# The opening of an adaLN block: Q/K weights loaded first, and chunk 2's norm, Q/K and values put elsewhere in the order

## The chip, the cores and the metric

The kernel runs on one core of one Trainium2 chip. The metric is the device time of one execution in microseconds (us), as the median of the runs. Before the change it is 575.89 us (three runs, 574.8 to 576.01).

## The reference

One transformer block on 2048 rows of 576 numbers: a modulation from a condition c, a local attention (32 heads of 18, 8 keys at a distance of 2 rows each), and a feed-forward of 4608 features. Cut to what matters:

```python
mod = (silu(c) @ w_mod).reshape(6, -1)           # sa, ca, ga, sb, cb, gb
h = layernorm(x) * (1 + ca) + sa
q, k, v = split(h @ wqkv)                        # 32 heads of 18
idx = pos - 2 * [0..7]                           # rows before 0 are masked
attn = softmax((q . k[idx]) * 18 ** -0.5)
x = x + ga * ((attn . v[idx]) @ wo)
h = layernorm(x) * (1 + cb) + sb
x = x + gb * (((h @ w_gate) * (h @ w_up)) @ w_down)
```

## The kernel before

The rows are cut into eight chunks of 256 (CH), each of two tiles of 128 rows (ST = 2). The feed-forward takes the 16 tiles in five groups (GROUPS): 2, 4, 4, 3 and 3 tiles. For each group `gate_up` walks through 36 feature blocks of 128 (FT) on TensorE, with the attention of later chunks as background pieces on the other engines, and `down` accumulates the output, with Q/K/V of later chunks between its matmuls.

The change is in what comes before the first `gate_up`, the opening. It has to bring the attention of chunk 0 to its end (x1, the second layernorm, and its transposed form h2T), the Q, K and V of chunks 1 and 2, and the modulation columns and rows. The order of work is written by hand (`manual_schedule` for all engines): each engine runs its instructions in the order in which the program issues them, and waits where an operand or a buffer isn't ready. So the order of the Python calls at lines 729 to 881 is the order of each engine's queue.

The names in that order:

- `load_x`, `load_k`, `load_wgu`, `load_res` (L130 to L169) issue DMAs on SP's queue. `wqk` holds the weights of Q and K, `wv` those of V. At L191 to L197 the queue has w_mod's first two blocks, x of chunk 1, `wv`, then `wqk`.
- `a_ln(i)` (L306) takes the layernorm sums of chunk i on VectorE (L233, L235); `aa[i]["rsq"]()` makes 1/sqrt on ScalarE (L238, L239); `aa[i]["norm"]()` normalizes on VectorE (L243); `a_norm(i)` is both. `a_t(i)` transposes the chunk on TensorE (L270) and applies the modulation while evicting (L259 on VectorE, L261 on ScalarE) into hT, of which there is one buffer.
- `a_qj(j, g, ...)` makes Q and K of tile j of chunk 0 (L338), in three groups of tiles: g = 0 is Q without its last tile, g = 1 the tile that Q and K share, g = 2 the rest of K. `a_q(i, g)` does so for both tiles of a later chunk in five groups. Both evict on ScalarE (L341 to L346). `a_v(i, j)` makes V (L364, L366), evicted on ScalarE (L368, L369). For later chunks it is written to the DRAM tile vd by POOL's queue (L375).
- `pj(j, w)` multiplies Q by the K that is shifted for window place w on VectorE (L761, six product buffers), `lj(j, w)` sums it by head on TensorE (L769); `max_j`, `sum_j` are the softmax (L775 to L777, L783 to L785).
- `to_keys(j)` turns the weights from queries to keys (L481, L484; copied by ScalarE, L487), `av_mul(j, hf)` weights V on VectorE (L496), `av_sum(j, hf)` sums with shifted matmuls into the three PSUM banks po (L507), copied to oT by ScalarE (L510 to L512).
- `b_wj(j)` is the output projection of tile j (L521); the function that it returns adds the residual and takes the sums of the second layernorm (L527, L528, L233). `rsq2`, `norm2` and `transposed(xn2, ...)` then make h2T, which the first gate/up matmuls (L621) read.
- `mod_columns(wmB, 1)` and `mod_row(...)` make modulation columns and the row of ga (L283; L295, L297, L298).
- `b_ld(i, j)` gathers the value rows of eight window places from vd into vsh, on POOL's queue (L383), `behind` makes it wait for the landing of a load of gate/up weights. The first group's `gate_up` reads chunk 1's vsh in its second half (L449).

PSUM has eight banks. In the opening, five are a rotating pool (psp0, `ps`), three hold po. When the opening ends both pools close, and a pool of all eight opens for `gate_up`.

Of the kernel before, what the change touches and what calls it, by code (L numbers as in the profile page):

```python
# [12 lines left out]
PSUM = bass.MemoryType.PSUM  # L13
# [6 lines left out]
D = 576  # L20
# [23 lines left out]
def kernel(  # L44
# [40 lines left out]
    wdp = pool("wdp", 3)  # L85
    gup = pool("gup", 3)
    outr = pool("outr", 1)
    guards = [tc.tile_pool(name="psp0", bufs=5, space=PSUM), tc.tile_pool(name="pop", bufs=3, space=PSUM)]
    psp, pop = [g.__enter__() for g in guards]

    def ps(shape, dt, name):
        return psp.tile(shape, dt, name=name, tag="bank")
# [1 line left out]
    def js(j):  # L94
        return slice(j * P, (j + 1) * P)
# [34 lines left out]
    def load_x(i):  # L130
        if i < NCH:
            x_in[i] = sp.tile([P, ST, D], BF, name="x_t1") if i == 1 else xin.tile([P, ST, D], BF, name="x_t")
            nc.sync.dma_start(x_in[i][:], x_rows(i))
# [32 lines left out]
    def load_k(dst, wsrc, c0, n):  # L166
        r = nc.sync.dma_start(dst(slice(0, P), slice(0, KF)), wsrc[0:KF * P, c0:c0 + n].rearrange("(k p) n -> p k n", p=P))
        nc.sync.dma_start(dst(slice(0, 64), KF), wsrc[KF * P:D, c0:c0 + n])
        return r  # L169
# [20 lines left out]
    nc.gpsimd.memset(wmCr[64:, :], 0.0)  # L190
    load_wm(wmA, 0, 0)  # L191
    load_wm(wmA, 1, 1)
    load_x(1)
    load_k(lambda p, k: wv[p, k, :], A_wqkv, 2 * D, D)
    load_k(lambda p, k: wqk[p, k, 0:D], A_wqkv, 0, D)
    load_k(lambda p, k: wqk[p, k, D:DP], A_wqkv, 2 * D - 64, 64)
    load_k(lambda p, k: wqk[p, k, DP:2 * D], A_wqkv, D, D - 64)  # L197


    nc.gpsimd.memset(ident[:], 0.0)  # L200
# [77 lines left out]
    def mod_columns(wm, pi):  # L278
        pm = ps([P, 2, KT], F32, "pm")
        for bi in range(2):  # L280
            for kt in range(KT):
                for m in range(KT):
                    nc.tensor.matmul(pm[:, bi, m:m + 1], lhsT=wm[:, kt, bi, col(m)], rhs=sc[:, kt:kt + 1],  # L283
                                     start=(bi == 0 and kt == 0 and m == 0), stop=(kt == KT - 1), skip_group_check=True)
        c01 = slice(2 * pi, 2 * pi + 2)
        nc.vector.tensor_tensor(modc[:, c01, 0:KF], pm[:, :, 0:KF], addc[:, :, 0:KF], ALU.add)
        for r in (slice(0, 64), slice(64, P)):
            nc.vector.tensor_tensor(modc[r, c01, KF:KT], pm[64:P, :, KF:KT], addc[64:P, :, KF:KT], ALU.add)
# [17 lines left out]
    def a_ln(i):  # L306
        x = x_in.pop(i)
        xn, rsq, norm = layernorm(lambda j: x[:, j, :], "a")
        aa[i] = dict(xn=xn, rsq=rsq, norm=norm)

    def a_norm(i):
        aa[i]["rsq"]()
        aa[i]["norm"]()
# [11 lines left out]
    def a_t(i, on_dve=True):  # L325
        a_tiles(i)
        hT = aa[i]["hT"]
        transposed(aa[i]["xn"], lambda m: hT[:, m, :], (0, 1), 0)(on_dve)
# [19 lines left out]
    def a_q(i, g):  # L348
        qk_tiles(i, QGRP[g], slice(0, CH), nc.scalar.copy)
        if g == 2:  # L350
            a_halo(i)

    def a_qj(j, g, evict):
        qk_tiles(0, QGRPJ[g], js(j), evict)
# [4 lines left out]
    def a_v(i, j):  # L359
        hT = aa[i]["hT"]  # L360
        pv = ps([P, VA * DH], F32, "pv")
        pvr = ps([P, VR * DH], F32, "pvr")
        for kt in range(KT):
            nc.tensor.matmul(pv[:], lhsT=hT[:, kt, js(j)], rhs=wv[:, kt, 0:VA * DH], start=(kt == 0), stop=(kt == KT - 1))  # L364
        for kt in range(KT):
            nc.tensor.matmul(pvr[:], lhsT=hT[:, kt, js(j)], rhs=wv[:, kt, VA * DH:D], start=(kt == 0), stop=(kt == KT - 1))  # L366
        v_sb = vstage.tile([P, DH, H], BF, name="v_sb")[:] if i else v0(j)
        nc.scalar.copy(v_sb[:, :, 0:VA], pv[:].rearrange("p (h d) -> p d h", d=DH))  # L368
        nc.scalar.copy(v_sb[:, :, VA:H], pvr[:].rearrange("p (h d) -> p d h", d=DH))  # L369
        r0 = HALO + i * CH + j * P  # L370
        if i == 0:
            if j == 1:
                nc.gpsimd.dma_start(vd[r0 + P - HALO:r0 + P, :], o_sbs[0][P - HALO:P, j, 0:D])
            return
        nc.gpsimd.dma_start(vd[r0:r0 + P, :], v_sb.rearrange("p d h -> p (d h)"))  # L375
# [116 lines left out]
    def av_mul(j, hf):  # L492
        if hf == 0:
            weighted.append(vshp.tile([P, W, DH, H], BF, name="vsh"))
        ws = slice(4 * hf, 4 * hf + 4)
        nc.vector.tensor_tensor(weighted[j][:, ws], v0(j)[:, None].to_broadcast([P, 4, DH, H]),  # L496
                                keyed[j][:, ws, None, :].to_broadcast([P, 4, DH, H]), ALU.mult)

    def av_sum(j, hf):
        if j == 0 and hf == 0:  # L500
            pos.extend(pop.tile([P, 2, CH], F32, name="po") for _ in range(3))
        v = weighted[j][:].rearrange("p w d h -> p w (d h)")
        r = DIL * (W - 1) if j == 0 else 0
        for w in range(4 * hf, 4 * hf + 4):
            sh = DIL * (W - 1 - w)
            for m in range(KT):
                nc.tensor.matmul(pos[m // 2][:, m % 2, j * P:(j + 1) * P + r], lhsT=v[:, w, col(m)], rhs=slide[:, P - sh:2 * P - sh + r],  # L507
                                 start=(j == 0 and w == 0 and m % 2 == 0), stop=(w == W - 1), skip_group_check=True)
        if hf == 1:
            nc.scalar.copy(oT[:, 0:2, js(j)], pos[0][:, :, js(j)])  # L510
            nc.scalar.copy(oT[:, 2:4, js(j)], pos[1][:, :, js(j)])
            nc.scalar.copy(oT[0:64, KF, js(j)], pos[2][64:P, 0, js(j)])  # L512
# [234 lines left out]
    mod_columns(wmA, 0)  # L747
    for e in ev:
        e()
    a_ln(1)  # L750
    for j in range(ST):
        for g in range(3):
            a_qj(j, g, nc.scalar.copy)

    prods, lgs = {}, {}
    dd0 = smp.tile([P, ST, W, H], F32, name="dd")
# [1 line left out]
    def pj(j, w):  # L758
        off = HALO - DIL * (W - 1 - w) + j * P
        prods[j, w] = prodp.tile([P, KT, P], BF, name="prodj", tag="prod")  # L760
        nc.vector.tensor_tensor(prods[j, w][:], aa[0]["qT"][:, :, js(j)], aa[0]["kT"][:, :, off:off + P], ALU.mult)  # L761

    def lj(j, w):
        if w == 0:
            lgs[j] = ps([P, W, H], F32, "lgj")
            if j == 0:
                nc.tensor.matmul(lgs[j][:], lhsT=ident[:], rhs=maskneg[:], start=True, stop=False, skip_group_check=True)
        for m in range(KT):
            nc.tensor.matmul(lgs[j][:, w, :], lhsT=prods[j, w][:, m, :], rhs=ind[:, m, :],  # L769
                             start=(m == 0 and j == 1), stop=(m == KT - 1), skip_group_check=True)  # L770

    def max_j(j):
        dd = dd0[:, j]
        mx = small.tile([P, H], F32, name="mxj")
        nc.vector.tensor_reduce(mx[:], lgs[j][:].rearrange("p w h -> p h w"), axis=AX.X, op=ALU.max)  # L775
        nc.vector.tensor_tensor(dd, lgs[j][:], mx[:, None, :].to_broadcast([P, W, H]), ALU.subtract)
        nc.scalar.activation(dd, dd, ACTF.Exp, scale=scale)  # L777
# [26 lines left out]
    for g in range(5):  # L804
        load_wgu(g)

    for w in range(2):
        pj(0, w)
    a_norm(1)
    for w in range(2, 4):  # L810
        pj(0, w)
    for w in range(4):
        lj(0, w)
        pj(0, w + 4)
    a_v(0, 0)
    for w in range(4, 8):
        lj(0, w)
    a_v(0, 1)
    for w in range(2):
        pj(1, w)  # L820
    max_j(0)
    for w in range(2, 4):
        pj(1, w)
    a_t(1, False)
    for w in range(4):
        lj(1, w)
    for w in range(4, 6):
# [1 line left out]
    sum_j(0)  # L829
    for w in range(6, 8):  # L830
        pj(1, w)
    a_q(1, 0)
    a_q(1, 1)
    for w in range(4, 8):
        lj(1, w)
    max_j(1)
    mod_columns(wmB, 1)
    a_q(1, 2)
    sum_j(1)
    a_q(1, 3)  # L840
    for j in range(ST):
        to_keys(j)
    av_mul(0, 0)
    a_q(1, 4)
    a_v(1, 0)
    av_mul(0, 1)
    av_sum(0, 0)
    a_v(1, 1)
    a_ln(2)
    aa[2]["rsq"]()  # L850
    av_sum(0, 1)
    av_mul(1, 0)
    aa[2]["norm"]()
    mod_row(lambda p, k: wmC[p, k, :] if k < KF else wmCr[p, :], ga_bc, sc_bc)
    x1_half = b_wj(0)
    av_sum(1, 0)
    av_mul(1, 1)
    a_t(2, False)
    xn2, stat2, rsq2, norm2 = ln_parts(lambda j: x1[0][j], "b")
    x1_half(stat2)  # L860
    rsq2(slice(0, 1))
    av_sum(1, 1)
    a_q(2, 0)
    x1_half = b_wj(1)
    behind(b_ld(1, 0), wgu_in[0])
    behind(b_ld(1, 1), wgu_in[1])
    x1_half(stat2)
    rsq2(slice(1, 2))
    norm2(0)
    ht, _ = h2_of(0)  # L870
    a_q(2, 1)
    transposed(xn2, lambda m: ht[:, m, js(0)], (0,), 2)()
    norm2(1)
    a_q(2, 2)
    a_q(2, 3)
    transposed(xn2, lambda m: ht[:, m, js(1)], (1,), 2)()
    a_q(2, 4)
    for j in range(ST):
        a_v(2, j)
    load_res(1)  # L880
    load_x(4)
    for guard in [sp_guard] + guards[::-1]:
# [73 lines left out]
```

## Time and profile before

| what | us |
|---|---|
| median of three runs | 575.89 |
| profiled execution | 575.69 |
| its span, first to last instruction | 573.7 |
| first Q/K matmul (L338) | 14.45 |
| first gate/up matmul (L621) | 63.06 |
| TensorE busy, whole span | 547.6 (95%) |
| VectorE, ScalarE, POOL busy | 327.1, 250.9, 67.2 |

The span in 40 slices of 14.3 us (busy tenths; 9 is 90% or more) shows the first four slices, the opening and a little more, apart from the rest:

```profile
PE   1897999999999999999999999999999999999996
DVE  5477679896667787343667777505727614322202
ACT  2354666444455555233255565131366611455500
PEclk9899999999999999999999999999999999999999
DMA  9999596958444665364433874338646665665063
```

The row PEclk is the clock that the throttle granted to TensorE. The DMA engines are full for the first four slices. Times of single events are us from the start of the span.

### The profile page before, as it was taken

To read this page: it belongs to the slowest core of one execution; us is meant where nothing else is said; L and a number is where in the kernel's file an instruction comes from. 1 tells how busy PE (TensorE), PEld (TensorE's weight loads), DVE (VectorE), ACT (ScalarE), POOL (GpSimd) and SP (SyncE) were. 2 spreads that over 40 slices of the span, in tenths; PEclk is the share of its full clock that TensorE was granted. 3 is DMA by queue.
4 is the path that set the end of the run, shared out by engine and by line. 5 is a ranking of instruction groups with operands and counts; after the bars stand their busy time and mean duration, and the time that the engine had idled before them with its cause. 6 is when DMAs were issued, how large, how long until landed. Compare 5 with 4: busy or idle time off the path is not lost.

```text
span 573.7 us, 14145 instructions
## 1 busy us (share of the span) xinstructions
PE 547.6 (95%) x5959; PEld 321.0 (56%) x5959; DVE 327.1 (57%) x787; ACT 250.9 (44%) x576; POOL 67.2 (12%) x103
## 2 busy tenths in 40 slices
PE   1897999999999999999999999999999999999996
PEld 1676888566444445656444444565556555565553
DVE  5477679896667787343667777505727614322202
ACT  2354666444455555233255565131366611455500
POOL 7001300222100100131100000122000022000020
PEclk9899999999999999999999999999999999999999
DMA  9999596958444665364433874338646665665063
GB/s 255 279 272 363 169 285 207 345 160 277 129 146 135 223 218 174 119 207 146 145 112 110 264 237 147 97 92 294 192 149 176 211 200 167 186 187 183 1 173 106
DMA packets 72303, 108.13 MB, mean 188 GB/s; under 512 B 4752, under 2 KB 62176, under 8 KB 72112
## 3 DMA queue, kind: packets, MB, share of 16 engines
q1 hardware_dynamic: 60464, 61.42, 35.3%
q0 software_dynamic: 11168, 45.81, 25.5%
q8 instruction: 46, 0.75, 0.6%
q14 instruction: 17, 0.14, 0.1%
q10 hardware_dynamic: 608, 0.00, 0.1%
HBM read 102.78 MB, written 4.44 MB: 187 GB/s over the span
## 4 chain that ended last, share of the span: by engine, by line
PE 82%; issue 3%; DMA 3%; DVE 0%; POOL 0%; ACT 0%; SPq 0%; POOLq 0%; DVEq 0%
PE pg L621 25%; PE acc L685 21%; PE pu L621 20%; PE pq L338 4%; PE accr L690 3%; PE pw L538 2%; PE pv L364 2%; PE lg L399 1%; DMA wd<-in_B_w_down_dram 1%; DMA wgu<-in_B_w_up_dram 1%; PE tr_pA L270 1%; PE oT_pA L469 0%; PE tr_pB L270 0%; PE pwr L536 0%; POOL vsh L383 0%
## 5 line engine op out<-in xcount | busy, mean ns | idle before, releaser
L621 PE MATMUL pg<-h2T,wgu 64*128 64x512 bf16 (+2 forms) x1440 | 277.3, 333 | 0.0
L621 PE MATMUL pu<-h2T,wgu 64*128 64x512 bf16 (+2 forms) x1440 | 276.0, 333 | 0.0
L621 PEld LDWEIGHTS <-wgu 64*128 64x128 bf16 x2880 | 141.4, 94 | 107.1 <-issue 0.5
L685 PE MATMUL acc<-wd,hh 128*128 128x512 bf16 x576 | 149.4, 380 | 0.5 <-DMA wd<-in_B_w_down_dram 0.4
L645 ACT CAST u_sb<-pu 128x512 bf16<-128x512 f32 (+2 forms) x180 | 90.1, 501 | 136.5 <-PE pg L621 133.1
L650 DVE TENSOR_TENSOR hh<-g_sb,u_sb 128x512 bf16<-128x512 bf16 (+2 forms) x180 | 66.2, 369 | 102.6 <-ACT g_sb L646 97.8
L690 PE MATMUL accr<-wd,hh 128*128 128x64 bf16 x576 | 101.0, 193 | 0.0
L646 ACT CAST g_sb<-pg 128x512 bf16<-128x512 f32 (+2 forms) x180 | 91.4, 508 | 0.0
L685 PEld LDWEIGHTS <-hh 128*128 128x128 bf16 x576 | 56.0, 98 | 62.7 <-issue 1.7
L164 POOL DMA_DIRECT2D wd<-in_B_w_down_dram x45 | 33.8, 752 | 282.7 <-PE accr L690 230.0
L621 PE MATMUL pg<-h2T,wgr 64*128 64x512 bf16 (+2 forms) x180 | 60.2, 335 | 0.6 <-ACT v_sb L369 0.6
L621 PE MATMUL pu<-h2T,wgr 64*128 64x512 bf16 (+2 forms) x180 | 60.2, 335 | 0.3 <-ACT u_sb L645 0.3
L690 PEld LDWEIGHTS <-hh 128*128 128x128 bf16 x576 | 52.4, 98 | 2.9 <-issue 0.9
L338 PE MATMUL pq<-hT,wqk 128*128 128x256 bf16 (+1 forms) x405 | 46.7, 268 | 5.0 <-DMA wqk<-in_A_wqkv_dram 4.3
L389 DVE TENSOR_TENSOR prod<-qT,kT 128x1280 bf16<-128x1280 bf16 x56 | 44.7, 818 | 2.8 <-PE lg L399 2.8
L338 PEld LDWEIGHTS <-wqk 128*128 128x128 bf16 x405 | 35.6, 102 | 11.4 <-DMA wqk<-in_A_wqkv_dram 4.3
L449 DVE TENSOR_TENSOR vsh<-vsh,attn 128x1152 bf16<-128x1152 bf16 x56 | 40.9, 750 | 0.0
L259 DVE TENSOR_SCALAR h2T<-tr_pA,modc 128x256 bf16<-128x256 bf16 (+1 forms) x30 | 9.7, 377 | 36.8 <-PE tr_pA L270 36.8
L383 POOL DMA_DIRECT2D vsh<-vd x14 | 12.6, 901 | 140.7 <-DVE o_sb L460 88.0
L621 PEld LDWEIGHTS <-wgr 64*128 64x128 bf16 x360 | 18.1, 94 | 17.3 <-issue 4.8
L341 ACT CAST qT<-pq 128x512 bf16<-128x512 f32 x16 | 9.3, 582 | 34.9 <-PE pq L338 34.9
L364 PE MATMUL pv<-wv,hT 128*128 128x504 bf16 x80 | 20.9, 395 | 0.0
(149 smaller groups left out, 435.6 us busy)
## 6 DMA issues: line engine op xcount, KB each, us to landing
wd<-in_B_w_down_dram POOLq DMA_DIRECT2D x45, 576.0 KB, 4.6
wgu<-in_B_w_gate_dram SPq DMA_DIRECT2D x45, 512.0 KB, 4.0
wgu<-in_B_w_up_dram SPq DMA_DIRECT2D x45, 512.0 KB, 5.2
vsh<-vd POOLq DMA_DIRECT2D x14, 1152.0 KB, 7.3
x_r<-in_A_x_dram SPq DMA_DIRECT2D x8, 288.0 KB, 6.3
out_dram<-x SPq DMA_DIRECT2D x16, 144.0 KB, 4.3
x_t<-in_A_x_dram SPq DMA_DIRECT2D x7, 288.0 KB, 6.3
vd<-v_sb POOLq DMA_DIRECT2D x14, 144.0 KB, 2.9
```

The costliest lines, as they stand in the source:

```text
L164: return nc.gpsimd.dma_start(wb[:], B_w_down[r0:r0 + FB * P, :].rearrange("(k p) n -> p k n", p=P))
L338: nc.tensor.matmul(pq[:, gi, :], lhsT=wqk[:, kt, m * P:(m + 1) * P], rhs=hT[:, kt, cols], start=(kt == 0), stop=(kt == KT - 1))
L364: nc.tensor.matmul(pv[:], lhsT=hT[:, kt, js(j)], rhs=wv[:, kt, 0:VA * DH], start=(kt == 0), stop=(kt == KT - 1))
L383: return nc.gpsimd.dma_start(vsh[:].rearrange("p w d h -> p w (d h)"), vsrc)
L389: nc.vector.tensor_tensor(prod[:], aa[i]["qT"][:], aa[i]["kT"][:, :, off:off + CH], ALU.mult)
L449: nc.vector.tensor_tensor(v, v, at, ALU.mult)
L621: return nc.tensor.matmul(bank[:, 0:N], lhsT=lhs, rhs=rhs, start=first, stop=last, skip_group_check=True)
L645: nc.scalar.copy(u[:, 0:N], pu[:, 0:N])
L646: nc.scalar.copy(g[:, 0:N], pg[:, 0:N])
L650: nc.vector.tensor_tensor(hh[:, f, 0:N], gu[0][:, 0:N], gu[1][:, 0:N], ALU.mult)
L685: nc.tensor.matmul(acc[j][:], lhsT=hh[:, f, js(j)], rhs=wb[:, f % FB, 0:512], start=(f == 0), stop=(f == FT - 1))
L690: nc.tensor.matmul(accr[:, j, :], lhsT=hh[:, f, js(j)], rhs=wb[:, f % FB, 512:D], start=(f == 0 and j == 0), stop=(f == FT - 1), skip_grou ...
```

## The change

The order of the opening is rewritten; no computation is added or left out. On SP's queue the six loads of `wqk` go ahead of x of chunk 1 and of `wv`. Q of both tiles of chunk 0 is made before K. The sums of chunk 1's layernorm come after chunk 0's Q/K, and its 1/sqrt directly behind them. V of chunk 0 is made early, ahead of chunk 1's transposes. Chunk 2's sums stand before the second softmax maximum, its norm before the second softmax sum, its transposes and ga's row before `to_keys`. The four `av_mul` follow each other but for Q/K groups of chunk 2 on TensorE. V of chunk 2 comes before the last transposes. The gathers of chunk 1's value rows are issued last, behind loads 3 and 4 of the gate/up weights and no longer 0 and 1. The three banks po are allocated below the five of psp0.

```diff
-    guards = [tc.tile_pool(name="psp0", bufs=5, space=PSUM), tc.tile_pool(name="pop", bufs=3, space=PSUM)]
-    psp, pop = [g.__enter__() for g in guards]
+    guards = [tc.tile_pool(name="pop", bufs=3, space=PSUM), tc.tile_pool(name="psp0", bufs=5, space=PSUM)]
+    pop, psp = [g.__enter__() for g in guards]
...
-    load_x(1)
-    load_k(lambda p, k: wv[p, k, :], A_wqkv, 2 * D, D)
     load_k(lambda p, k: wqk[p, k, 0:D], A_wqkv, 0, D)
     load_k(lambda p, k: wqk[p, k, D:DP], A_wqkv, 2 * D - 64, 64)
     load_k(lambda p, k: wqk[p, k, DP:2 * D], A_wqkv, D, D - 64)
+    load_x(1)
+    load_k(lambda p, k: wv[p, k, :], A_wqkv, 2 * D, D)
...
+    for j, g in ((0, 0), (1, 0), (0, 1), (0, 2), (1, 1), (1, 2)):
+        a_qj(j, g, nc.scalar.copy)
     a_ln(1)
-    for j in range(ST):
-        for g in range(3):
-            a_qj(j, g, nc.scalar.copy)
+    aa[1]["rsq"]()
...
-    for w in range(2):
+    for w in range(3):
         pj(0, w)
-    a_norm(1)
-    for w in range(2, 4):
+    aa[1]["norm"]()
+    for j in range(ST):
+        a_v(0, j)
+    for w in range(3, 6):
         pj(0, w)
+    a_t(1, False)
     for w in range(4):
         lj(0, w)
-        pj(0, w + 4)
-    a_v(0, 0)
+    for w in range(6, 8):
+        pj(0, w)
+    a_q(1, 0)
     for w in range(4, 8):
         lj(0, w)
-    a_v(0, 1)
-    for w in range(2):
+    for w in range(4):
         pj(1, w)
     max_j(0)
-    for w in range(2, 4):
-        pj(1, w)
-    a_t(1, False)
+    a_q(1, 1)
+    a_q(1, 2)
     for w in range(4):
         lj(1, w)
     for w in range(4, 6):
...
-    a_q(1, 0)
-    a_q(1, 1)
+    a_q(1, 3)
     for w in range(4, 8):
         lj(1, w)
+    a_ln(2)
+    aa[2]["rsq"]()
     max_j(1)
+    a_q(1, 4)
     mod_columns(wmB, 1)
-    a_q(1, 2)
+    aa[2]["norm"]()
     sum_j(1)
-    a_q(1, 3)
+    for j in range(ST):
+        a_v(1, j)
+    a_t(2, False)
+    mod_row(lambda p, k: wmC[p, k, :] if k < KF else wmCr[p, :], ga_bc, sc_bc)
     for j in range(ST):
         to_keys(j)
     av_mul(0, 0)
-    a_q(1, 4)
-    a_v(1, 0)
     av_mul(0, 1)
+    a_q(2, 0)
     av_sum(0, 0)
-    a_v(1, 1)
-    a_ln(2)
-    aa[2]["rsq"]()
+    av_mul(1, 0)
+    a_q(2, 1)
     av_sum(0, 1)
-    av_mul(1, 0)
-    aa[2]["norm"]()
-    mod_row(lambda p, k: wmC[p, k, :] if k < KF else wmCr[p, :], ga_bc, sc_bc)
+    av_mul(1, 1)
+    xn2, stat2, rsq2, norm2 = ln_parts(lambda j: x1[0][j], "b")
+    ht, _ = h2_of(0)
+    av_sum(1, 0)
     x1_half = b_wj(0)
-    av_sum(1, 0)
-    av_mul(1, 1)
-    a_t(2, False)
-    xn2, stat2, rsq2, norm2 = ln_parts(lambda j: x1[0][j], "b")
     x1_half(stat2)
     rsq2(slice(0, 1))
+    a_q(2, 2)
     av_sum(1, 1)
-    a_q(2, 0)
+    norm2(0)
+    a_q(2, 3)
     x1_half = b_wj(1)
-    behind(b_ld(1, 0), wgu_in[0])
-    behind(b_ld(1, 1), wgu_in[1])
     x1_half(stat2)
     rsq2(slice(1, 2))
-    norm2(0)
-    ht, _ = h2_of(0)
-    a_q(2, 1)
     transposed(xn2, lambda m: ht[:, m, js(0)], (0,), 2)()
     norm2(1)
-    a_q(2, 2)
-    a_q(2, 3)
-    transposed(xn2, lambda m: ht[:, m, js(1)], (1,), 2)()
     a_q(2, 4)
     for j in range(ST):
         a_v(2, j)
+    transposed(xn2, lambda m: ht[:, m, js(1)], (1,), 2)()
+    behind(b_ld(1, 0), wgu_in[3])
+    behind(b_ld(1, 1), wgu_in[4])
     load_res(1)
     load_x(4)
```

## The prediction

> **What bounds the kernel now.** The first view to read is that of the waits of TensorE (PE). From 62 us to the end it has 1.8 us in all:
>
> ```profile
> PE pg L621 <- ACT v_sb L369: 0.6, 1, 0.6
> PE pwr L536 <- ACT oT L470: 0.5, 1, 0.5
> PE acc L685 <- DMA wd<-in_B_w_down_dram: 0.4, 1, 0.4
> PE pu L621 <- ACT u_sb L645: 0.3, 1, 0.3
> ```
>
> So from the first gate/up matmul (L621, at 63.06) on, PE sets the time, and whatever moves that start moves the end. The opening before it is the opposite. The same view up to 63.05, longest waits:
>
> ```profile
> PE tr_pA L270 <- DVE ln_xn L243: 7.7, 2, 6.3
> PE pq L338 <- DMA wqk<-in_A_wqkv_dram: 4.3, 1, 4.3
> PE lgj L769 <- DVE prodj L761: 2.4, 1, 2.4
> PE pwj L521 <- ACT oT L510: 1.9, 1, 1.9
> ```
>
> The 4.3 is Q/K's wait for weights, which ends at 14.45. Busy time by stretch (length, then PE, PEld, DVE, ACT, POOL, granted clock, DMA share, GB/s) says what limits what follows:
>
> ```profile
> 14.44:21.36 6.92, 6.91 (x94) 6.83 (x95) 0.89 (x2) 2.81 (x7) 0.00 (x0) 1.00 1.10 306
> 21.36:31.20 9.84, 6.83 (x93) 4.18 (x92) 7.48 (x20) 3.85 (x11) 0.66 (x1) 0.83 1.10 238
> 31.20:38.34 7.14, 6.55 (x131) 5.97 (x130) 4.88 (x14) 3.69 (x10) 0.00 (x0) 1.00 1.03 250
> 38.34:46.45 8.11, 8.11 (x89) 6.05 (x88) 8.04 (x14) 4.23 (x13) 1.11 (x2) 1.00 1.09 353
> 46.45:52.54 6.09, 4.17 (x62) 3.64 (x60) 3.20 (x9) 2.29 (x7) 1.81 (x2) 1.00 1.09 366
> 56.20:63.06 6.86, 5.91 (x56) 4.45 (x57) 4.18 (x12) 5.73 (x16) 0.57 (x1) 1.00 0.36 126
> ```
>
> PE alone in Q/K; then VectorE (DVE) and PE by turns; in the last stretch ScalarE (ACT) is near full, and its timeline shows the end of the opening:
>
> ```profile
> 56.64 0.57 ACT L341 CAST qT<-pq 128x512 bf16<-128x512 f32 x1
> 57.10 0.81 ACT L261 ACTIVATE h2T<-tr_pB,modc 128x128 bf16<-128x128 bf16 x2
> 57.94 0.37 ACT L343 CAST kT<-pq 64x256 bf16<-64x256 f32 x1
> ...
> 62.31 0.58 ACT L368 CAST v_sb<-pv 128x504 bf16<-128x504 f32 x1 [0.53 <-PE pv L364]
> 62.78 0.23 ACT L369 CAST v_sb<-pvr 128x72 bf16<-128x72 f32 x1
> ```
>
> Chunk 2's Q/K and V evictions stand there behind the last layernorm and end at 63.01.
>
> **The change, step by step.** I walk the new order through the engines; every duration is start to next start in the timelines of before. "(before x)" is the same event there.
>
> 1. Q/K weights first. 288 KB of x1 and 648 KB of wv leave the place before them: 0.96 MB at 340 to 299 GB/s (slices 5 to 10 and 10 to 15 us) is 2.8 to 3.2 us; I take 3.0, so Q starts at 11.45 (before 14.45). Its hT tiles are there: DVE evicts from 10.80, ACT is done at 11.95. The cost falls on what moved back: 1.33 MB of wqk passes x1, which lands at 10.3 + 4.3 = 14.6; its sums (1.9) end at 16.5, under Q/K. wv lands ahead of x2, whose place in the queue is unchanged (12.2 + 5.5 = 17.7); it is needed at 18.2. Were it 2 us later still, a_v(0) would only meet the transposes that wait for chunk 1's norm until 20.6.
>
> 2. Q/K, 90 matmuls. PE runs slow at first, though the clock column has 1.00 there:
>
> ```profile
> 14.40:16.40 2.00, 1.95 (x19) 1.00 1.09 308
> 18.00:20.00 2.00, 2.00 (x38) 1.00 1.09 330
> ```
>
> 36 in 2 us (less two that straddle) is 0.056 each, so the last 56 fill 18.05 to 21.18 and the first 34 took 3.6 us. With the same 34 slow, Q/K takes 6.7 and ends at 18.2. K of tile 0 is now complete at the 65th matmul (16.8), not the 45th; with 0.87 for its eviction DVE's first product starts at 17.6 (before 19.48). Norm(1) starts 1.25 after Q/K's end, at 19.43 (before 22.43).
>
> 3. DVE to max(0): three products to 18.8, wait, norm(1) 1.09, three products 1.24, two hT tiles 0.73, six products 2.47: 24.95 (before 27.51). PE beside it: both a_v(0) 2.46 to 20.6, transposes, four logits, Q(1,0) behind ACT's three hT tiles to 23.7; nothing later than DVE.
>
> 4. max(0) 0.84, two products 0.85, sum(0) 1.34, two products 0.85: 28.85. Chunk 2's layernorm sums (L233, L235) come here, 1.9, then max(1) 0.84: 31.6 (before 34.96).
>
> 5. PE goes on from the last logits at 29.0: Q/K(1,4) 1.09, mod_columns 1.25, both a_v(1) 2.46, chunk 2's transposes 0.55, ga's row (mod_row) 1.23: 35.6, then to_keys. ACT is last here: v's eviction to 34.5, hT(2) 1.47, ga 0.6, keyed 0.4. The first av_mul starts at 37.0 (before 38.34), the smallest gain of all steps. DVE has done norm(2) and sum(1) by 34.7.
>
> 6. Four av_mul of 1.27 with no layernorm between (before 3.2 us of it): 42.1 (before 46.45). PE: Q(2,0) to 37.3, av_sum(0,0) 38.4 to 39.6, Q(2,1) 1.09, av_sum(0,1) to 42.0. av_sum(1,0) writes the same po banks and so waits for ACT's oT copies (0.92): ends at 43.85. b_wj(0) follows, and DVE adds x1's first tile from 44.7 (before 48.94), 2.72, to 47.4.
>
> 7. ACT: rsq 0.44, Q/K(2,2)'s evictions 0.81 (new in this place), oT(1) from 48.65 (before 52.13); b_wj(1) on PE waits for it, and behind b_wj(1) stand the transposes of x1's first tile. DVE's second tile starts 1.30 behind, 49.95, ends at 52.7; rsq done at 53.2 (before 56.64).
>
> 8. ACT's tail: h2T(0) 0.84, K 0.53, two v of 0.62, h2T(1) 0.82: 3.4 us, where before 6.4 remained, because most Q/K(2) evictions are done by then. PE is done with its transposes at 55.2. First gate/up matmul: 56.6 (before 63.06).
>
> Priced at nothing: the exchange of the PSUM pools (gate/up's first banks are then po's, free since ACT's oT copies); mod_row and the two load orders on SP behind them (wmC lands at 19.6 + 8.7 = 28.3, needed at 34.4). The value-row gathers (L383) move on POOL's queue behind chunk 2's vd writes, 47.3 to 56.5, and with them wm5 and the first two wd are issued 4.2 us earlier instead of 6.45. They are read from 87.4 - 6.45 = 81 on; their landings took 9.5 and 10.7 us, so they are there by 70.
>
> Sum: 63.06 - 56.6 = 6.45 us. The profiled execution took 575.69 (span 573.7, 2.0 around it), 0.2 under the median of 575.89. Against the median: **569.4**.
>
> **Rivals.**
> (a) The slow clock lasts longer. If it is released at 18.05 again, whenever Q starts, 62 matmuls run slow and Q/K ends 1.45 later: 570.9. Or it returns at the end of the opening: before, PE idled 2.4 of the 3.5 us up to 24.87 and then the trace has
>
> ```profile
> 24.87:28.28 3.41, 3.41 (x33) 1.79 (x32) 2.69 (x7) 0.70 (x2) 0.00 (x0) 0.50 1.15 306
> ```
>
> The new order closes that gap, but in the 3.4 us before 56.6 PE idles 2.1 (behind h2T evictions). Half clock over 3.41 us costs up to 1.7: 571.1. Against it: 46.45 to 52.54 idled 1.9 of 6.1 without a drop. [...]
> (b) ACT gives the gain back at step 5. It is full there; if the copies ahead of keyed slip by another 1.3, av_mul starts where it did, and of the later gains only the 3.2 us of layernorm taken out of av_mul stays: 572.7.
> (c) Slower: the gathers' 2.36 MB now come together with wm5 and two wd (1.84 MB, as before) and the first refilled weights, wgu of the 21st feature block (1.05 MB, issued 4.7 us after the first gate/up matmul: 61.3). PE reads these at 85.45 - 6.45 = 79.0 (its timeline has that block's first matmul at 85.45) and stops until they have landed. That makes 5.25 MB from 56.5 on. At the 350 GB/s that the stretches with gathers show (366, 361) they take 15 us and land at 71.5. The kernel is slower from a landing after 85.5 on, a mean rate under 181 GB/s; at the 126 GB/s of the last stretch above, the lowest while gathers were under way, they land at 98 and the time is 588. But that stretch ran out of requests, so I give it little.
> (d) The order does nothing (a wait that I don't see holds 63.06): 575.9.
>
> **How the numbers follow.** The walk 0.49, (a) 0.26, (b) 0.14, (c) 0.04, (d) 0.02, and 0.05 for more gain (a slow stretch of 2 us instead of 3.6 gives 0.8, weights 3.2 us earlier 0.2: 568.4, and 568 with a little more). Range: 567.8 to 572.8; it takes in the weights' bounds (0.2 either way), both forms of (a), and (b). About 0.2% (1.2 us) can be told from no change: faster 0.94, same 0.02, slower 0.04.
>
> **What would show it.** The first L338 matmul at 11.2 to 11.7; the first L761 product at 17.6; L775 near 25.0 and 30.8; the first L496 at 37.0, four in a row; the first L527 at 44.7; the first L621 at 56 to 57 released by h2T L261; PE's waits after it still under 2 us. Wrong if L621 starts on time and PE then waits for wgu or vsh, if a 0.50 clock appears after 18 us, or if L496 starts after 38.

## The result, and the profile after

The changed kernel takes 569.37 us (median of six runs, 568.46 to 570.24) beside 575.91 for the kernel before (six runs as well): a ratio of 0.9892, 95% interval 0.9873 to 0.9911. Its profiled execution took 570.18 us with a span of 568.1, 5.6 us less than the profile before.

Waits of TensorE (PE), profile after, from the last wait of the opening to the end (total us, times, longest):

```profile
PE pg L621 <- ACT h2T L261: 1.2, 1, 1.2
PE accr L690 <- DMA wd<-in_B_w_down_dram: 0.7, 1, 0.7
PE pwr L536 <- ACT oT L470: 0.5, 1, 0.5
PE pu L621 <- ACT u_sb L645: 0.3, 1, 0.3
PE acc L685 <- DMA wd<-in_B_w_down_dram: 0.2, 1, 0.2
```

The first line is the end of the opening, released by h2T and no longer by a value eviction. Behind it PE still waits for next to nothing, for no gate/up weight and no gathered value row. The same view up to 57.1 us:

```profile
PE tr_pA L270 <- DVE ln_xn L243: 6.3, 1, 6.3
PE pq L338 <- DVE hT L259: 1.3, 1, 1.3
PE pg L621 <- ACT h2T L261: 1.2, 1, 1.2
PE pwj L521 <- ACT oT L510: 1.1, 1, 1.1
```

The 4.3 us for wqk is gone. In this execution Q/K's last wait, 1.25 us, is for hT; in e12 below, the same kernel, it is for wqk again, 1.45 us. The 2.4 for products is 0.5, the second wait for a layernorm (7.7 in two before) is gone. Busy time by stretch, ending at Q/K's end, 28.0, the first av_mul, the first and second L527, and the first L621 (length, then PE, PEld, DVE, ACT, POOL, granted clock, DMA share, GB/s):

```profile
11.07:19.18 8.11, 8.10 (x91) 7.85 (x92) 3.64 (x12) 3.33 (x9) 0.79 (x1) 1.00 1.09 338
19.18:28.00 8.82, 8.45 (x124) 6.64 (x123) 8.22 (x23) 5.78 (x15) 0.65 (x1) 1.00 1.11 270
28.00:37.45 9.45, 8.86 (x153) 6.70 (x151) 7.66 (x25) 6.00 (x18) 1.12 (x2) 1.00 1.04 258
37.45:45.14 7.69, 6.59 (x83) 5.66 (x81) 5.16 (x5) 2.31 (x6) 0.00 (x0) 1.00 1.10 361
45.14:50.46 5.32, 4.22 (x47) 3.32 (x46) 3.20 (x10) 2.46 (x9) 0.00 (x0) 1.00 1.03 329
50.46:56.89 6.43, 4.94 (x46) 3.34 (x45) 5.16 (x16) 3.79 (x12) 1.01 (x2) 1.00 0.05 17
```

Right behind Q/K PE and DVE are both above 93%, where before (21.36 to 31.20) they had 69% and 76%. ACT has room in the last stretch (3.79 of 6.43 us busy, before 5.73 of 6.86), because Q/K(2)'s evictions are mostly done by then. Its last piece of work there is h2T, from 55.97 on.

One thing went worse. Q/K ran from 11.08 to 19.17, 8.09 us for what took 6.89 before. Two stretches of 2 us inside it, PE alone:

```profile
11.10:13.10 2.00, 2.00 (x19) 1.00 1.09 322
17.10:19.10 2.00, 2.00 (x38) 1.00 1.08 347
```

19 against 38 matmuls is half clock against full; the trace's clock records begin at 17.08, so 6.0 us were slow, not 3.6. The start of gate/up gained 6.17 us (63.06 to 56.89). Of this 0.82 is missing later: from the first L621 of group 2 (273.23) to that of group 3 (398.08) the profile after has 124.85, the one before 124.03; the 0.7 us wait for wd above (L690) lies there.

### The profile page after: what moved, and what is told of

The parts are those of the page before. It is cut to its first block, busy times and chain, and to the rows that moved or that the text cites. A ratio compares the mean times of both kernels' runs of the same rounds, so it can differ in the third digit from the quotient of the medians.

```text
span 568.1 us, 14147 instructions
## 1 busy us (share of the span) xinstructions
PE 547.8 (96%) x5959; PEld 321.6 (57%) x5959; DVE 327.4 (58%) x787; ACT 250.4 (44%) x576; POOL 67.2 (12%) x103
## 4 chain that ended last, share of the span: by engine, by line
PE 83%; DMA 6%; issue 4%; DVE 2%; ACT 2%; POOL 1%; SPq 0%; POOLq 0%; DVEq 0%
PE pg L621 25%; PE pu L621 20%; PE acc L685 19%; PE pq L338 6%; DMA wd<-in_B_w_down_dram 3%; PE accr L690 3%; PE pv L364 2%; PE pw L538 2%; DMA wgu<-in_B_w_up_dram 2%; PE lg L399 2%; DMA wmA<-in_w_mod_dram 1%; DMA vd<-v_sb 1%; PE po L507 1%; PE tr_pA L270 1%; ACT hT L261 0%
## 5 line engine op out<-in xcount | busy, mean ns | idle before, releaser
L621 PE MATMUL pg<-h2T,wgu 64*128 64x512 bf16 (+2 forms) x1440 | 277.3, 333 | 0.0
L621 PE MATMUL pu<-h2T,wgu 64*128 64x512 bf16 (+2 forms) x1440 | 276.0, 333 | 0.0
L621 PEld LDWEIGHTS <-wgu 64*128 64x128 bf16 x2880 | 141.3, 94 | 107.2 <-issue 0.5
L690 PE MATMUL accr<-wd,hh 128*128 128x64 bf16 x576 | 101.0, 193 | 0.7 <-DMA wd<-in_B_w_down_dram 0.7
L621 PE MATMUL pg<-h2T,wgr 64*128 64x512 bf16 (+2 forms) x180 | 60.2, 335 | 1.2 <-ACT h2T L261 1.2
L621 PE MATMUL pu<-h2T,wgr 64*128 64x512 bf16 (+2 forms) x180 | 60.2, 335 | 0.3 <-ACT u_sb L645 0.3
L690 PEld LDWEIGHTS <-hh 128*128 128x128 bf16 x576 | 52.5, 98 | 3.5 <-issue 1.4
L338 PE MATMUL pq<-hT,wqk 128*128 128x256 bf16 (+1 forms) x405 | 48.0, 273 | 1.6 <-DVE hT L259 1.3
L621 PEld LDWEIGHTS <-wgr 64*128 64x128 bf16 x360 | 18.0, 94 | 17.9 <-issue 5.5
L456 DVE TENSOR_TENSOR vsh<-vsh 128x1152 bf16<-128x1152 bf16 x28 | 20.5, 751 | 0.0
```

Source lines behind the costliest of these rows:

```text
L338: nc.tensor.matmul(pq[:, gi, :], lhsT=wqk[:, kt, m * P:(m + 1) * P], rhs=hT[:, kt, cols], start=(kt == 0), stop=(kt == KT - 1))
L456: nc.vector.tensor_tensor(vsh[:, d], vsh[:, d], vsh[:, 4 + 2 * s:6 + 2 * s], ALU.add)
L621: return nc.tensor.matmul(bank[:, 0:N], lhsT=lhs, rhs=rhs, start=first, stop=last, skip_group_check=True)
L690: nc.tensor.matmul(accr[:, j, :], lhsT=hh[:, f, js(j)], rhs=wb[:, f % FB, 512:D], start=(f == 0 and j == 0), stop=(f == FT - 1), skip_grou ...
```

## The experiments

Twelve kernels were run, each beside runs of the kernel before. One table holds what they rest on. "Slow" is the time from the first Q matmul to the release of the clock; the last column, first L621 less Q/K's end, takes the draw of the slow stretch out. (e4 had the full clock for one step before Q/K; its 3.1 runs to the second release.) Times are from each kernel's profile, ratios from its runs.

| kernel | ratio to before (95%) | Q start | slow | Q/K end | first L621 | behind Q/K |
|---|---|---|---|---|---|---|
| before | 1 | 14.45 | 3.6 | 21.34 | 63.06 | 41.72 |
| changed | 0.9892 (0.9873 to 0.9911) | 11.08 | 6.0 | 19.17 | 56.89 | 37.72 |
| changed again (e12) | 0.9877 (0.9859 to 0.9895) | 11.65 | 2.7 | 18.10 | 55.81 | 37.71 |
| e1 | 0.9953 (0.9934 to 0.9971) | 14.29 | 6.0 | 22.32 | 60.67 | 38.35 |
| e2 | 0.9965 (0.9953 to 0.9977) | 10.99 | 5.5 | 18.86 | 60.41 | 41.55 |
| e3 | 0.9951 (0.9939 to 0.9963) | 10.57 | 3.7 | 17.57 | 60.20 | 42.63 |
| e4 | 0.9890 (0.9877 to 0.9903) | 11.56 | 3.1 | 18.22 | 56.06 | 37.84 |
| e5 | 0.9926 (0.9914 to 0.9939) | 11.64 | 5.9 | 19.64 | 59.40 | 39.76 |
| e6 | 0.9853 (0.9835 to 0.9870) | 11.38 | 0 | 16.84 | 55.03 | 38.19 |
| e7 | 0.9909 (0.9896 to 0.9923) | 11.47 | 3.5 | 18.30 | 58.54 | 40.24 |
| e8 | 0.9868 (0.9854 to 0.9883) | 11.33 | 3.8 | 18.31 | 55.50 | 37.19 |
| e9 | 0.9883 (0.9858 to 0.9908) | 10.85 | 4.0 | 17.98 | 55.69 | 37.71 |
| e10 | 0.9849 (0.9830 to 0.9868) | 10.92 | 0 | 17.89 | 55.07 | 37.18 |
| e11 | 0.9880 (0.9862 to 0.9897) | 10.52 | 6.0 | 18.55 | 56.26 | 37.71 |

A ratio step of 0.001 is 0.58 us. Differences between two kernels are read against both runs of the changed one, 0.9892 and 0.9877; a range given so leaves out the ratios' own intervals, which are 0.7 to 1.4 us either way.

**e1_weights_back**

```diff
+    load_x(1)
+    load_k(lambda p, k: wv[p, k, :], A_wqkv, 2 * D, D)
     load_k(lambda p, k: wqk[p, k, 0:D], A_wqkv, 0, D)
...
-    load_x(1)
-    load_k(lambda p, k: wv[p, k, :], A_wqkv, 2 * D, D)
```

> The changed kernel with one part undone: x(1) and wv are again loaded ahead of the Q/K weights; every engine's order stays the new one. Theory (the end of the Q/K stretch is carried to the end): the first Q matmul goes back from 11.08 to about 14.45 us, but the slow clock then covers only about 3.6 us of the stretch and not 6.0, as in the kernel before, so Q/K ends at about 21.3 in place of 19.0, the first L621 comes at about 59.1 in place of 56.9, and the time is 571.4 to 571.8. Rival 1 (the start of Q/K is what counts, 3.37 later): 572.7. Rival 2 (later stages have slack and swallow most of it, as they swallowed 0.56 of the 0.85 us by which Q/K ended later than I had worked out): 569.9 to 570.3.

Median 572.78; by the ratios 3.5 to 4.4 us slower than the changed kernel. Q starts 3.21 later, the slow stretch is as long as in the changed kernel, and Q/K ends 3.15 later. Rival 1 holds. The premise of my theory, that a later start has the shorter slow stretch, fell. The other 0.63 of L621's 3.78 us appears between the second softmax and the first av_mul, where PE stood 0.5 us at mod_columns (L283) without a wait that the profile shows.

**e2_weights_only** (the kernel before, with the loads' order alone)

```diff
-    load_x(1)
-    load_k(lambda p, k: wv[p, k, :], A_wqkv, 2 * D, D)
     load_k(lambda p, k: wqk[p, k, 0:D], A_wqkv, 0, D)
...
+    load_x(1)
+    load_k(lambda p, k: wv[p, k, :], A_wqkv, 2 * D, D)
```

> The kernel before with one part of the change alone: the Q/K weights are loaded ahead of x(1) and wv; every engine keeps the old order. Theory (two parts of about equal size, which add): Q/K starts at about 11.1 in place of 14.45 and ends about 2.3 us earlier, the first product moves with it, and the time is about 573.6 (573.0 to 574.0). Rival 1 (the loads carry nearly all of it): 569.5 to 570.5. Rival 2 (in the old order the norm of chunk 1 and the V weights, which now land later, take the place of what is won): 575.5 to 576.

573.40, as the theory has it: 2.0 us by the ratio (1.3 to 2.7). Q/K ends 2.48 earlier and gate/up starts 2.65 earlier; what lies behind Q/K takes 41.55 (before 41.72). So the loads alone are worth 2.0 us and the order alone 2.7 (e1), where both together gave 6.2 to 7.1. In the traces, with the Q/K stretch left out, the parts do add: Q starts 0.16 us earlier in e1 and 3.46 in e2, what lies behind Q/K is 3.37 and 0.17 shorter, 7.2 in all; the changed kernel has 3.37 and 4.00, 7.4. Whether the ratios would add with many more runs stays open. e2's clock fell twice behind its release, in the profile before once (24.87):

```profile
23.32:26.74 3.42, 3.42 (x41) 0.50 1.08 279
50.63:54.04 3.41, 3.41 (x19) 0.50 1.05 357
```

(Length, PE busy, granted clock, DMA share, GB/s.)

**e3_tail_back**

```diff
     norm2(1)
+    transposed(xn2, lambda m: ht[:, m, js(1)], (1,), 2)()
     a_q(2, 4)
     for j in range(ST):
         a_v(2, j)
-    transposed(xn2, lambda m: ht[:, m, js(1)], (1,), 2)()
```

> The changed kernel with the last step alone undone: a_q(2,4) and the two a_v(2) stand again behind the transposes of tile 1, between them and gate/up. Theory (work that PE does while ACT and DVE make the second half of h2T covers that wait): the first L621 moves from 56.9 to about 58.3 and the time to 570.8 (570.3 to 571.3). Rival (ACT's copies between the norm and h2T set the end of this stretch, whichever order PE has them in): 569.4, within 0.3. Rival (ACT reaches h2T sooner when the K and V copies stand behind it): 568.5.

572.76: 3.4 to 4.3 us slower than the changed kernel, over twice what I expected; in the trace 4.9 behind Q/K's end. PE idled 2.98 us ahead of the last transposes, the clock fell at 51.80, and what was now behind the transposes ran at half speed: the K group of ten matmuls, 1.25 us in the changed kernel, in the timeline:

```profile
53.21 2.34 PE L338 MATMUL pq<-hT,wqk 128*128 128x256 bf16 x10
```

and PE's busy time and granted clock over the four us from there:

```profile
53.21:57.21 4.00, 4.00 (x17) 0.50 0.00 0
```

**e5_tail_fill** (e3, with the idle time filled)

```diff
     norm2(1)
+    fill = pop.tile([P, 2, CH], F32, name="po")
+    for _ in range(46):
+        nc.tensor.matmul(fill[:, 0, 0:P], lhsT=ident[:], rhs=ident[:], start=True, stop=True)
     transposed(xn2, lambda m: ht[:, m, js(1)], (1,), 2)()
```

> The kernel of e3 (a_q(2,4) and a_v(2) behind the last transposes) plus 46 matmuls of the identity with itself, into a PSUM tile that nobody reads, in the 2.98 us that PE idled there ahead of the last transposes. In e3's profile the clock fell to 0.50 at 51.80 us and the 25 matmuls behind it took some 2.0 to 2.6 us longer than in the changed kernel's profile. Theory (the step is worth its 3.4 us for two reasons: about 2.9 of work that then follows the norm, and the rest a clock that falls while PE idles): no record of 0.50 in this stretch, the last a_q takes 1.25 in place of 2.34, and the time is 0.3 to 1.5 below e3's 572.8, so 571.3 to 572.5, still 2 to 3 above the changed kernel. Rival 1 (order alone: the fall of the clock is an accident of that one profile): 572.8 within 0.3. Rival 2 (the clock is most of it): 569.4 to 570.5.

571.82, and the same K group:

```profile
55.07 1.25 PE L338 MATMUL pq<-hT,wqk 128*128 128x256 bf16 x10
```

The clock did not fall (1.00 from 51.68 to 55.10). From the last transposes to L621 it took 4.62 us (54.78 to 59.40), in e3 7.50 (52.70 to 60.20). The theory holds, with other sizes: of e3's 4.9 us, 2.9 is the clock and 2.0 (39.76 less 37.72) the order. But 2.9 is that profile's share: it lists a mean granted clock of 0.994, e3's other four runs 0.996 to 0.998. By the ratios the fill is worth 1.4 us against e3, and e5 stays 2.0 to 2.8 behind the changed kernel.

**e4_warm** and **e6_warm_full** (PE kept busy ahead of Q/K; e6's 12 matmuls stand between the two halves of `mod_columns`; `warm(n)` is n matmuls like those of e5)

```diff
+    warm(30)
     ev = [transposed(xn0, lambda m, j=j: hT0[:, m, js(j)], (j,), 0) for j in range(ST)]
-    mod_columns(wmA, 0)
+    mod_columns(wmA, 0)                  # e4
+    warm(14)                             # e4
+    mod_columns(wmA, 0, 12)              # e6
+    warm(24)                             # e6
```

> The changed kernel plus 44 matmuls of the identity with itself into a PSUM tile that nobody reads: 30 ahead of the first transposes (from about 3 us) and 14 between the mod columns and Q/K. Theory (the 6.0 us of slow matmuls in Q/K are the price that the earlier start pays; a PE that is busy from 3 us on has the clock released before 11 us): Q/K takes 5.0 us in place of 8.1 and ends at about 16.1, x(1) and wv then hold back a part, the first L621 comes 1.5 to 2.5 us earlier and the time is 566.9 to 567.9. Rival 1 (the release comes at a fixed time, or not by PE's own work): 569.4, and the slow matmuls are still there. Rival 2 (Q/K is faster, but x(1), wv and the norm of chunk 1 hold all of it back): Q/K ends at about 16 and the time is 569 to 569.5.

569.07, a ratio within the interval of the changed kernel: the theory's time missed, since Q/K still had slow matmuls. PE by clock step:

```profile
4.43:7.84 3.41, 3.41 (x41) 1.00 1.04 347
7.84:11.25 3.41, 2.06 (x58) 1.00 1.12 294
11.25:14.66 3.41, 3.10 (x30) 0.50 1.10 327
```

The first step was full and released the clock; the second held waits of 1.0 and 0.65 us, and 44 of its 58 matmuls were the one-column ones of `mod_columns` (L283); it lost the clock again, just ahead of Q/K. e6 closes these waits too:

> The changed kernel plus matmuls of the identity with itself wherever PE idles ahead of Q/K: 30 ahead of the first transposes, 12 between the halves of the mod columns, 24 behind them. In e4's profile the clock was released at 7.84, fell at 11.25 and was released again at 14.66; the stretch 7.84 to 11.25 held two waits and 50 one-column matmuls. Theory (records come in steps of 3.41 us whose start is not tied to the program, and a step has to be busy from end to end): no fall at 11 us, Q/K has no slow matmul, takes 5.0 us from about 11.3 and ends at 16.3 in place of 19.2, and since e3's and e4's profiles carried every us of Q/K's end on to max(0) one for one, the time is 566.6 to 567.6, unless wv or x(1) hold it back by up to 1 (then 567.6 to 568.4). Rival 1 (one-column matmuls never count as busy, so the clock falls as in e4): 569.0. Rival 2 (the end of Q/K is not on the path): 569.4 with a Q/K that ends before 17.

567.21, a ratio of 0.9853: 1.4 to 2.2 us faster than the changed kernel and inside the theory's range, though x(1) held back a part. No matmul of Q/K was slow (90 in 5.46 us, in the changed kernel 8.09), and it ended at 16.84. The first product came at 17.06 behind x(1)'s sums, which is why 38.19 is left behind Q/K's end.

**e7_ln2_back**

```diff
-    a_ln(2)
-    aa[2]["rsq"]()
     max_j(1)
...
-    aa[2]["norm"]()
     sum_j(1)
...
     av_sum(0, 0)
-    av_mul(1, 0)
-    a_q(2, 1)
+    a_ln(2)
+    aa[2]["rsq"]()
     av_sum(0, 1)
+    av_mul(1, 0)
+    aa[2]["norm"]()
+    mod_row(lambda p, k: wmC[p, k, :] if k < KF else wmCr[p, :], ga_bc, sc_bc)
     av_mul(1, 1)
+    a_t(2, False)
+    a_q(2, 0)
```

> The changed kernel with chunk 2's norm undone: its sums stand between the weighted sums, its norm, the row of gates and its transposes behind them, and its five Q/K groups follow from there on. Theory (between the softmaxes the norm fills waits of DVE; among the products it takes about 2 us of DVE on the path, of which an earlier first product gives about 1 back): 570.4 (569.9 to 571.4). Rival 1 (the change's gain at this place is most of what the order brought): 572.6. Rival 2 (it moves work without changing the sum): 569.4.

570.98, inside the theory's range; 1.0 to 1.8 us slower than the changed kernel by the ratios, 2.5 in the trace behind Q/K's end. The first av_mul is 1.96 nearer to Q/K's end (34.62 less 18.30, against 37.45 less 19.17), and the first L527 is 1.93 further from it (46.20). Taking the layernorm out of the av_mul stretch wins 3.9 us there and costs 2.0 ahead of it.

**e8_keys_first**

```diff
-    mod_row(lambda p, k: wmC[p, k, :] if k < KF else wmCr[p, :], ga_bc, sc_bc)
     for j in range(ST):
         to_keys(j)
+    mod_row(lambda p, k: wmC[p, k, :] if k < KF else wmCr[p, :], ga_bc, sc_bc)
```

> The changed kernel with the two to_keys ahead of the row of gates, so that on ACT the keyed copies, which the first product waits for, stand ahead of the two ga_bc copies (0.57 us). Theory (ACT's copies are last there, and what the first product wins is carried on one for one): the first L496 moves from 37.45 to 36.9 and the time to 568.8 (568.6 to 569.1). Rival (to_keys waits for attn, or the oT copies are last later on, so nothing is won): 569.4.

568.50. Behind Q/K's end the first av_mul gains 0.60 (35.99 less 18.31) and L621 0.53. The two ga copies were on the path, as step 5 had it. The ratio's 0.5 to 1.4 us does not exclude the theory's 0.6.

**e9_unpriced_back**

```diff
-    guards = [tc.tile_pool(name="pop", bufs=3, space=PSUM), tc.tile_pool(name="psp0", bufs=5, space=PSUM)]
-    pop, psp = [g.__enter__() for g in guards]
+    guards = [tc.tile_pool(name="psp0", bufs=5, space=PSUM), tc.tile_pool(name="pop", bufs=3, space=PSUM)]
+    psp, pop = [g.__enter__() for g in guards]
...
     x1_half = b_wj(1)
+    behind(b_ld(1, 0), wgu_in[0])
+    behind(b_ld(1, 1), wgu_in[1])
...
-    behind(b_ld(1, 0), wgu_in[3])
-    behind(b_ld(1, 1), wgu_in[4])
```

> The changed kernel with the two parts undone that I had priced at nothing: the PSUM pools are allocated in the old order, and chunk 1's two row gathers are issued ahead of the last norm, behind the first two gate/up blocks, in place of the fourth and fifth. Theory (neither ends a wait of PE): within 0.4 of the changed kernel's time in this call. Rival (one of them carries part of the gain): 0.6 or more slower.

0.9883 beside 0.9877 for the changed kernel run with it (e12). The ratio's interval is 1.4 us either way and can't tell the rival's 0.6; the trace can. It has the same 37.71 behind Q/K's end, and behind L621 PE waits 1.2 us in all (e12 1.1), so neither part carries anything there.

**e10_best** (e6 and e8 together, and `load_x(1)` between the Q and the K weights)

```diff
     load_k(lambda p, k: wqk[p, k, D:DP], A_wqkv, 2 * D - 64, 64)
+    load_x(1)
     load_k(lambda p, k: wqk[p, k, DP:2 * D], A_wqkv, D, D - 64)
-    load_x(1)
```

> The kernel of e6 (PE kept busy ahead of Q/K) with the keys first as in e8, and with x(1) loaded ahead of the K weights in place of behind them. In e6's profile Q/K ended at 16.84, but the first product stood behind x(1)'s sums until 17.06, and x(1) landed at 15.15. Theory (gains on one chain add): the sums are done before K of tile 0 is (about 16.1), so the first product gains 0.9, the keyed copies 0.55, and the time is 565.8 (565.2 to 566.5). Rival 1 (a_v(0) waits for wv, which landed at 17.15 in e6, and takes back what x(1) gives): 566.6. Rival 2 (the K weights now land too late for Q/K): 567.2 or more.

567.41, no better than e6: rival 2. PE's waits from 10.5 to 20 us (L345 is the Q/K matmul in this kernel):

```profile
PE pq L345 <- DMA wqk<-in_A_wqkv_dram: 1.2, 2, 1.1
```

The K weights, put back by x(1), are now late, and Q/K ends at 17.89 in place of 16.84. The keys' 0.53 is there (37.18). The fastest kernels of this study are e6 and e10, both faster than the changed one and than the one before.

**e11_tiles_back**

```diff
-    for j, g in ((0, 0), (1, 0), (0, 1), (0, 2), (1, 1), (1, 2)):
+    for j, g in ((0, 0), (0, 1), (0, 2), (1, 0), (1, 1), (1, 2)):
```

> The changed kernel with one part undone: Q/K goes tile by tile again (Q and K of tile 0, then of tile 1) in place of Q of both tiles first. The first product then waits for 45 matmuls and not for 65. Theory (the products start about 1.2 earlier, but PE has all of Q/K, a_v(0) and the transposes to do before the logits, so only a part is won): first product at about 5.0 us after Q's start at full share, max(0) 0.3 to 0.8 earlier against the end of Q/K, and 0.3 to 0.8 faster than the changed kernel in this call. Rival 1 (DVE's products set the pace): 1.1 to 1.4 faster. Rival 2 (the order makes no difference to the end): within 0.2.

0.9880 beside 0.9877 (e12): rival 2. The first product came 5.64 us after Q's start (7.35 in the changed kernel, with an equally long slow stretch), yet max(0) stands 6.45 behind Q/K's end in both (25.00 less 18.55, 25.62 less 19.17). The reason stands in VectorE's own order. Behind the third product comes chunk 1's norm (L243), which needs its 1/sqrt, and ACT makes that behind its copies of Q/K's last group. So the norm starts 1.08 and 1.09 us behind Q/K's end, and VectorE then works without a gap to max(0). The norm in e11 and in the changed kernel:

```profile
19.63 1.19 DVE L243 TENSOR_SCALAR ln_xn<-x_t,ln_mva,ln_rstda 128x576 bf16<-128x576 bf16 x4 [2.18 <-ACT ln_rstda L239]
20.26 1.19 DVE L243 TENSOR_SCALAR ln_xn<-x_t,ln_mva,ln_rstda 128x576 bf16<-128x576 bf16 x4 [0.53 <-ACT ln_rstda L239]
```

What the products gained became a longer wait. No run moved the 1/sqrt ahead of these copies.

**e12_after_again** (the changed kernel, unchanged)

> The changed kernel itself, once more, beside the others of this call. Theory (the stretch of slow matmuls at the start of Q/K lasts from 3.4 to 6.8 us, by where the 3.41 us steps of the clock happen to stand, and half of it is lost; the 0.8 us of waits for wd in the down product of group 2 also come in some executions only): median 569.4 within 0.5, single runs spread over some 1.7 us, and a profile with another length than 6.0 us. Rival (both belong to the changed kernel): the same 6.0 us and the same waits in this profile as in the first.

569.38, and the theory holds on both counts but for its lower bound: the slow stretch took 2.7 us, under the 3.4, and from group 2 to group 3 it was 124.02 us, so the 0.82 us of waits for wd did not come back. Its L621 stands where the first profile has it behind Q/K's end, 37.71.

## Why the prediction was right, step by step

The forecast was 569.4 and the kernel takes 569.4, but two halves of the sum, Q/K's end and what lies behind it, were off in opposite directions. That the median came within 0.1 us is luck; the runs of the changed kernel lie between 568.3 and 570.2.

One thing about the count first. The walk takes Q/K's end as the place where the next matmul could start (18.18; before 21.18). The table takes the end of the last matmul in the profile, 0.16 later (before 21.34). On the table's count the walk's end of Q/K is 18.34, and the figures of the walk below are counted from there.

- **Step 1, weights first.** Q was to start at 11.45; the profiles with the new load order have 10.5 to 11.7, with the last word at hT in the changed kernel's first profile and at wqk in e12. e1 shows that the loads make the difference (14.29 without them), and e2 that it is carried on.
- **Step 2, Q/K.** This is the mis-sized term: "with the same 34 slow" took one profile's 3.6 us for a property of the kernel. It was 6.0 in the changed profile, Q/K ended at 19.17 in place of 18.34, and this half gave 2.17 instead of 3.00. Rival (a), a longer slow stretch, came true in that execution. In e12 it was 2.7 us, Q/K ended at 18.10, and the half gave 3.24. By the runs the stretch is a draw. The kernel before should draw too, which would mostly leave the ratio of the medians alone; that is argued, since it has one profile.
- **Step 3, DVE to max(0).** The interval from Q/K's end, 6.61 by the walk, was 6.45, and the mechanism is the walk's. The norm starts 1.09 behind Q/K's end in the walk and in the profile, and "nothing later than DVE" holds: VectorE goes from the norm to max(0) without a gap (e11), and PE's last logits end 0.5 us ahead of max(0). That the first product now waits for the 65th matmul cost nothing. Where x(1) is late (e6), its sums set the time in place of the norm's 1/sqrt.
- **Steps 4 and 5.** From Q/K's end, max(1) came at 12.10 (walk 12.41) and the first av_mul at 18.28 (18.66), 0.3 and 0.4 early. ACT is last there (e8), and rival (b), that it takes more, is refuted.
- **Steps 6 and 7.** First L527 25.97 behind Q/K's end (26.36), the second 31.29 (31.61). e7 puts the moved layernorm at 2.5 us.
- **Step 8, the tail.** 37.72 behind Q/K's end for L621 (38.26). So everything behind Q/K gained 4.00 us, not the 3.46 that the walk gives. Up to the first av_mul the new order even takes 1.28 us longer, as it holds chunk 2's layernorm there; from the first av_mul to L621 it takes 5.28 less. The tail's order is worth 2.0 at full clock (e5), and it also keeps PE busy enough: with the old order the clock could fall there (e3), which my 3.4 us of ACT copies did not contain.
- **The clock behind Q/K.** The second form of rival (a), a fall of the clock at the end of the opening, is in neither profile of the changed kernel, and its ten runs list a mean granted clock of 0.997 to 0.999. Of the 33 runs of the kernel before that were made beside the experiments, 23 list 0.995 or less. The fall behind the last matmul explains 0.003 of that at most (up to 2.95 us at half in the fourteen profiles). So most executions of the kernel before lose the clock at least once where the changed kernel keeps it; what that is worth in the medians was not separated.
- **Priced at nothing.** Right: e9. Rival (c) is refuted by the waits after L621, rival (d) by its start and by the time.

In the profiled pair 2.17 and 4.00 make 6.17. The first group of the feed-forward gave 0.22 more (84.11 us for 84.33) and the stretch with the wd wait took 0.82 back, which leaves the 5.6 of the spans. In e12 3.24 and 4.01 make 7.25, and its span is 7.4 below the one before (566.3 against 573.7).

## What to carry to other kernels

Before a duration from one profile goes into a sum, ask whether it belongs to the kernel or to that execution; where a clock is involved, split the trace at an event behind it (here Q/K's end) and compare the two sides apart. Moving work ahead of a wait pays twice when it also keeps TensorE's clock up: the idle time in e3 cost 2.9 us of clock in its profile, 1.4 by the ratios of e3 and e5. An earlier start for one engine is worth nothing if the next instruction in its own order waits for an event that did not move (e11), and an earlier operand is worth nothing if another one now comes last (e10).

## What the runs showed of the hardware

- **The clock moves in steps of 3.41 us that are not tied to the program.** A slow stretch at the same place of the program was 2.7 to 6.0 us long in eleven profiles (e4, e6 and e10 apart). In the two profiles of the changed kernel it was 6.0 and 2.7, with the full clock from 17.08 and from 14.31 on. About half of it is lost: 19 matmuls in 2 us there, 38 behind it (changed kernel). Within a profile the changes of the clock stand whole steps apart (before: 18.04, 24.87, 28.28).
- **A step need not be full to release it, and 1.8 us of idle time in a step was enough to lose it (e2).** It was released after a step with 2.66 of 3.41 us busy (e12) and not after 2.59 (the changed kernel). It fell after steps with 0.93 (before), 1.33 (e3), 1.50 and 1.62 us busy (e2), and stayed after 1.86 (before), 1.93 (e9), 1.95 (e10) and 2.03 (e7). The steps in e12 and before (length, PE busy, granted clock, DMA share, GB/s):

```profile
10.90:14.31 3.41, 2.66 (x26) 1.00 1.09 323
48.76:52.17 3.41, 1.86 (x21) 1.00 1.11 370
```

- **Steps with one-column matmuls do not fit these numbers.** With 50 of them and 10 transposes, a step with 2.66 us busy in e1 (below) and one with 2.73 in e2 released nothing: the first clock records there come at 20.24 and 16.50. In e4 the clock fell after 2.06 us, more than in steps that kept it; 44 of its 58 matmuls had one column, and its longest single wait was 1.0 us. Whether these matmuls are the reason is not separated by a run.

```profile
6.59:10.00 3.41, 2.66 (x60) 1.00 1.07 344
```

- **The weights' landing in the down product varies.** The 0.82 us from group 2 to group 3 came in two of fourteen profiles (the changed kernel and e2, 124.85 each, with a 0.7 us wait for wd in both); in the others that interval was 124.0 to 124.2.
